# Two re-orderings in a fused attention + FFN kernel: x transposes in 64-token halves, and a second numerator among the gate/up chunks

## The chip, the cores and the metric

The kernel runs on one core of a Trainium2 chip. The metric is the device time of one execution in microseconds (us), lower is better; the figure given is the median of three runs. TensorE (PE) does the matmuls and, as a matmul against an identity, transposes; its weight loads are listed separately as PEld. VectorE (DVE), ScalarE (ACT) and GpSimd (POOL) do the elementwise work; SyncE (SP) issues DMAs in order.

## The reference

With x of 2048 tokens by 640 channels, 32 heads of 20 channels:

```
g   = sigmoid((x * gate_w).sum(-1))
q,k,v = x @ wqkv;  pq = q @ w_phi,  pk = k @ w_phi          (per head)
phi(y) = concat(softmax(y), softmax(-y))                     (40 features a head)
kv  = sum_s phi_k[s] v[s]^T,   z = sum_s phi_k[s]            (no mask: one state for all tokens)
o   = (phi_q @ kv) / (phi_q . z + 1e-6)
a   = o @ wo
b   = (gelu(x @ w_gate) * (x @ w_up)) @ w_down               (F = 1728)
out = g * a + (1 - g) * b
```

All tensors are bf16, sums are kept in f32 in PSUM.

## The kernel before

The 2048 tokens are 16 tiles of 128 tokens, and 4 blocks of 4 tiles. PSUM has 8 banks; the order of the work on each engine is written out by hand, and a small recording layer (`_Sched`) puts in the semaphore waits that the reads and writes of each operation ask for. Nothing is reordered by a planner: an engine's program order is the order in which the Python code calls it.

The stages, in the order in which PE goes through them:

1. **Start (`attention_state`, lines 544 to 572).** Seven matmuls on a constant, then the transposes of the first x block. The four tiles of that block are loaded token-major into `xtok` by two DMAs of two tiles each (line 216). `x_transpose` (line 289) transposes one tile: five PE transposes of 128 tokens by 128 channels (line 293) into one PSUM bank, then one copy to `xT`, on DVE (line 301) or ACT (line 299). Tiles 0 to 3 use banks 6, 7, 2, 3 and are copied by DVE, ACT, DVE, DVE. Then `v_step` (line 363) makes the value projection of these four tiles, one 128-row slice of `wv` at a time: for each slice and tile a matmul of 480 and one of 160 columns (line 366). It writes bank t and bank 4 or 5. The five slices of `wv` come by five DMAs (line 236), queued on SP behind the two of `xtok`.
2. **Attention state (up to line 621).** The feature weights are folded into the projections, and keys, values and queries of all tiles are made; `gram` sums the state over tiles.
3. **Gate/up (`gateups`, line 791).** For each block 14 chunks of 128 FFN channels. A chunk is 5 matmuls of 512 columns for gate and 5 for up (line 354), then gelu on ACT (line 642) and the product on DVE (line 644). Two pairs of banks, (0,1) and (6,7), alternate.
4. **Down (`downs`, line 797).** For each block two pairs of tiles (`down_pair`, line 705). A pair sums `hT @ w_down` and `goT @ wo` of two tiles in the two 64-row halves of the array at the same time: half r works on tile r first and then on the other tile, so that no two halves write one bank at once. In the first half of a pair ("opening") row r goes over all 14 down chunks and the 5 `wo` chunks of its tile, for each of the column parts of the output, in the second ("closing") over 13 down chunks and the 5 `wo` chunks of the other tile. A step (a `yield`) is two matmuls, one a half.

Between these steps stand the **numerators**: `num(t)` (line 660) makes the attention output of tile t. It is 20 matmuls of 88 columns in 64-row halves (line 670) into banks 2 to 5, then eleven DVE operations (lines 686 to 699) and a transposing DMA on SP from `Og` to `goT` (line 702). The `wo` matmuls of tile t wait for that DMA. In gate/up the DVE operations of a numerator stand in DVE's program order between two products of line 644, and these set free the banks that PE writes next.

In the kernel before, `num(0)` stands after the fifth chunk of the second gate/up block (`first_nums`, line 819). `num(1)` to `num(5)` stand in the first down block, after its steps 1, 31, 61, 91 and 121; the other three down blocks hold 4, 4 and 2 numerators at steps 1, 31, 61, 91. The first pair of the first block has an order of its own (`late`, line 766): all down legs of both halves come first, and the `wo` legs of all column parts last. There, a leg that enters a bank waits on the semaphore that the leg of the other half raises when it leaves it (`enter`, `leave`, `("turn", bk)` in line 728 and 729).

Of the kernel before, what the change touches and what calls it, by code (L numbers as in the profile page):

```python
# [3 lines left out]
P = 128  # L4
BF16 = mybir.dt.bfloat16
F32 = mybir.dt.float32
AF = mybir.ActivationFunctionType
# [100 lines left out]
class _Kernel:  # L108
# [6 lines left out]
    NFC = 14  # L115
# [170 lines left out]
        for s in range(self.NSV):  # L286
            pool(lambda e, s=s: e.memset(self.vaug[:, s, :, DH:self.DA], 1.0), [("vone", s)])

    def x_transpose(self, t, b, ek):
        sc = self.sc  # L290
        pv = self.bank(b).bitcast(BF16)
        for c in range(self.KD):
            sc.op("pe", lambda e, c=c: e.transpose(
                pv[:, c * P:(c + 1) * P], self.xtok[:, t, c * P:(c + 1) * P], self.ident[:, :]),
                reads=[("xtok", t), "ident"], writes=[("ps", b)], signal=(c == self.KD - 1))
        out = self.xT[:, :, t * P:(t + 1) * P]
        src = pv[:, 0:self.D].rearrange("p (c t) -> p c t", t=P)
        if ek == "a":
            sc.op("act", lambda e: e.activation(out, src, AF.Copy), reads=[("ps", b)], writes=[("xT", t)])
        else:  # L300
            sc.op("dve", lambda e: e.tensor_copy(out, src), reads=[("ps", b)], writes=[("xT", t)])

    def blockdiag(self):
        DH = self.DH
# [239 lines left out]
    def attention_state(self):  # L544
        NT = self.NT
        order = [(b, i) for b in range(self.NB) for i in range(self.KD)]
        sc = self.sc
        ones = self.nc.const_aps.tensor(1.0, [P, 512], BF16)
        for n in (512, 512, 512, 512, 512, 512, 128):
            sc.op("pe", lambda e: e.matmul(self.bank(0, n), ones[:, 0:P], ones[:, 0:n], start=True, stop=True),  # L550
                  writes=[("ps", 0)])
        vs, ve, xt = self.v_step, self.v_first_evac, self.x_transpose
        xt(0, 6, "d")
        xt(1, 7, "a")
        xt(2, 2, "d")
        xt(3, 3, "d")
        for t in range(4):
            vs(t, 0)
        for t in range(4):
            vs(t, 1)  # L560
        for t in range(4):
            vs(t, 2)
        for t in range(4):
            vs(t, 3)
        self.blockdiag()
        self.gate_column(6)
        for t in range(4):
            vs(t, 4)
            ve([t], "ad"[t % 2], False)
            if t == 2:  # L570
                ve([0, 1, 2], "a", True)
        ve([3], "d", True)
        f = self.fold
        ve, ke = self.v_early, self.k_early
        ve(4, 6)
        ve(5, 0)
        f(0, "k", (2, 3), "d")
        f(1, "k", (4, 5), "a")
        f(2, "k", (6, 7), "d")
        f(3, "k", (0, 1), "a")  # L580
        f(4, "k", (2, 3), "d")
        ve(6, 4)
        ke(0, 6)
        self.k_sums(0)
        ve(7, 0)
        ke(1, 2)
        f(0, "q", (4, 5), "d")
        f(1, "q", (6, 7), "d")
        ke(2, 0)
        f(2, "q", (4, 5), "d")  # L590
        f(3, "q", (2, 3), "d")
        self.proj(3, 640, 384, 6, 128, ["wk2"])
        f(4, "q", (4, 5), "d")
        self.proj(3, 1024, 257, 7, 0, ["wk2", "wgate"])
        self.k_evac(3, 6)
        self.k_scale(0)
        self.k_norm(1)
        self.pq(0, 1, 1, 0)
        self.pq(0, 0, 0, 1)
        self.pq(0, 3, 3, 2)  # L600
        self.columns = True
        self.gram(0)
        self.k_norm(2)
        self.pq(0, 2, 2)
        self.k_norm(3)
        n = 4
        g = 1
        for t in range(4, NT):
            if t < 8:
                self.k_early(t, 1)  # L610
            else:
                self.vk(t)
            self.k_norm(t)
            m = 2 * t - 2 if t < 8 else t + 5
            while n < m:
                if n == m - 1:
                    for g in range(g, t - 2):
                        self.gram(g)
                    g = t - 2
                self.pq(order[n][0], order[n][1], n)  # L620
                n += 1
# [80 lines left out]
        sc.dma("sp", lambda e: e.dma_start_transpose(self.goT[:, gs, :, :], self.Og[:, sl, :]),  # L702
               reads=[("Og", sl)], writes=[("goT", gs)], guard=old)

    def down_pair(self, t0, banks, widths, late):

        sc = self.sc
        ts = (t0, t0 + 1)
        NFC, KD = self.NFC - 1, self.KD
        nw = len(widths)  # L710
# [1 line left out]
        last = t0 + 2 == self.NT  # L712
        os_ = t0 % 4

        def mm(r, j, h, c, start, stop, enter, leave):
            t = ts[j]
            tt, gs, bk, w0, a = t % 4, t % 8, banks[h][j], sum(widths[:h]), 64 * r
            w = widths[h]
            if c <= NFC:
                lhs, rhs = self.hT(hk, c)[a:a + 64, tt * P:(tt + 1) * P], self.wd_sb[a:a + 64, c, w0:w0 + w]  # L720
                rd = [("hT", hk, c), "wd"] if c < NFC else [("hT", hk, 13, r), ("wd13", r)]
            else:
                k = c - NFC - 1
                lhs, rhs = self.goT[a:a + 64, gs, k, :], self.wo_sb[a:a + 64, k, w0:w0 + w]
                rd = [("goT", gs), "wo"]
            sc.op("pe", lambda e: e.matmul(self.bank(bk, w), lhs, rhs, start=start, stop=stop,  # L726
                                           skip_group_check=True),
                  reads=rd, writes=[("ps", bk)] + ([("turn", bk)] if leave else []), signal=leave,
                  after=[("turn", bk)] if enter else ())

        def evac(h):
            w0, w = sum(widths[:h]), widths[h]
# [18 lines left out]
                   reads=[("outsb", os_ + j, k) for j in (0, 1) for k in hs], writes=[("out", t0, h)])  # L751

        wos = [NFC + 1 + k for k in range(KD)]
        down = (list(range(NFC + 1)), list(range(NFC)))

        def leg(h, half, cs, first, fin, enter, leave):

            for x, c in enumerate(cs):
                for r in (0, 1):
                    mm(r, (r, 1 - r)[half], h, c, first and x == 0, fin and x == len(cs) - 1, enter and x == 0,  # L760
                       leave and x == len(cs) - 1)
                if fin and x == len(cs) - 1:
                    evac(h)
                yield None

        if late:
            for half in (0, 1):
                for h in range(nw):
                    yield from leg(h, half, down[half], half == 0, False, half == 1, True)
            for h in range(nw):  # L770
                yield from leg(h, 0, wos, False, False, True, True)
                yield from leg(h, 1, wos, False, True, True, True)
        else:
            for h in range(nw):
                yield from leg(h, 0, down[0], True, False, False, False)
            for h in range(nw):
                yield from leg(h, 0, wos, False, False, False, True)
            for h in range(nw):
                yield from leg(h, 1, down[1] + wos, False, True, True, True)

    NUMB = 2
    oldk = [("Ek", k, r) for k in range(4) for r in (0, 1)] + [(w, k) for w in ("Dk", "Rk") for k in range(4)] + [
# [3 lines left out]
    def ffn(self):  # L786
        self.gn = 0
        self.pn = 0
        pairs = [(0, 1), (6, 7)]

        def gateups(b, after):
            for idx, c in enumerate([0, 1, 13] + list(range(2, 13))):
                self.gateup(b, c, pairs[self.pn % 2])
                self.pn += 1
                after(idx)

        def downs(b, side):
            p = [pairs[(self.pn + k) % 2] for k in (0, 1)]
            n = 0
            for t in (4 * b, 4 * b + 2):  # L800
                final = t + 2 == self.NT
                for _ in self.down_pair(t, p + [(2, 3)] if final else p, (256, 256, 128) if final else (320, 320),
                                        t == 0):
                    n += 1
                    if n in side:
                        self.num(side[n])

        def state(idx):
            if idx < 3:
                self.gram(13 + idx)  # L810
            if idx == 2:
                self.columns = False
                self.kv_evac()
                self.gates()
                self.kv_ones()
            if 6 <= idx < 11:
                self.kv_mask(idx - 6)

        def first_nums(idx):
            if idx == 4:  # L820
                self.num(0)

        def none(idx):
            pass
        at = (1, 31, 61, 91, 121)
        nums = ((1, 2, 3, 4, 5), (6, 7, 8, 9), (10, 11, 12, 13), (14, 15))
        gateups(0, state)
        gateups(1, first_nums)
        gateups(2, none)
        gateups(3, none)  # L830
        for b in range(self.NB):
            downs(b, dict(zip(at, nums[b])))


def bass_gated_mix__linear_kernel_hedgehog__geglu_ffn__prompt_kernel(
# [41 lines left out]
```

## Time and profile before

| | us |
|---|---|
| median of three runs (290.58 to 292.26) | 290.98 |
| the profiled execution | 290.58 |
| its span, first to last instruction | 289.2 |
| PE busy (98% of the span) | 283.3 |
| DVE busy (61%) | 175.1 |
| ACT busy (36%) | 104.6 |
| down matmuls of line 726, `w_down` part, 320 columns, x648 | 48.8 |
| numerator matmuls of line 670, x320 | 9.0 |
| first transposes, line 293, x20 | 2.0 |

Rows of the profile read: the line of the kernel, the engine, the operation, what is written from what, and the tile shape; then the busy time. Matmuls overlap in the array, so the mean time of one (296 ns for a matmul of 320 columns) is longer than the time from the start of one to the start of the next. "Idle before" names the wait that ended last before an instruction started. The table of windows gives each engine's busy time and number of instructions in a stretch of the span.

### The profile page before, as it was taken

How to read it: one execution, taken by the hardware profiler on the slowest of the kernel's cores; microseconds unless marked ns; L12 is line 12 of the kernel's file. 1: busy time of each engine (PE TensorE's matmuls, PEld its weight loads, DVE VectorE, ACT ScalarE, POOL GpSimd, SP SyncE). 2: the span in 40 equal slices, each digit the busy share in tenths (PEclk: the TensorE clock that was granted, in tenths of full speed). 3: DMA queues.
4: the chain of work that ended last, by engine and by line, in shares of the span. 5: the costliest groups of instructions: out<-in, count | busy, mean ns of one | idle time of the engine just before them, and what ended most of it. 6: DMA issues, size and time to landing. Idle time of an engine off the chain costs nothing. (4 is left out here: it accounts for less than half of the span.)

```text
span 289.2 us, 7022 instructions
## 1 busy us (share of the span) xinstructions
PE 283.3 (98%) x3032; PEld 186.3 (64%) x3032; DVE 175.1 (61%) x353; ACT 104.6 (36%) x199; POOL 5.3 (2%) x36
## 2 busy tenths in 40 slices
PE   8999999999999999999999999999889999999996
PEld 4666799999984444444444444446557777777785
DVE  2359999999976644643232324236686884884801
ACT  3367888667844233222332232320112022022021
POOL 7000000000000000000000000000000000000000
DMA  7999996000002000010000000000221322532221
GB/s 225 204 184 215 370 366 196 2 0 2 0 2 48 0 0 0 3 24 0 2 0 0 0 2 0 0 0 2 48 71 25 93 44 74 70 43 76 70 71 48
DMA packets 36937, 18.67 MB, mean 65 GB/s; under 512 B 28970, under 2 KB 36394, under 8 KB 36906
## 3 DMA queue, kind: packets, MB, share of 16 engines
q1 hardware_dynamic: 36240, 18.19, 25.8%
q8 instruction: 24, 0.39, 0.6%
q10 hardware_dynamic: 666, 0.03, 0.2%
q14 instruction: 7, 0.06, 0.1%
HBM read 9.04 MB, written 2.62 MB: 40 GB/s over the span
## 5 line engine op out<-in xcount | busy, mean ns | idle before, releaser
L354 PE MATMUL ps<-xT,wg_sb 128*128 128x512 bf16 (+1 forms) x270 | 64.9, 379 | 0.0
L354 PE MATMUL ps<-xT,wu_sb 128*128 128x512 bf16 (+1 forms) x270 | 64.8, 379 | 0.0
L642 ACT ACTIVATE gl<-ps 128x512 bf16<-128x512 f32 x52 | 30.9, 597 | 72.4 <-PE ps L354 70.3
L644 DVE TENSOR_TENSOR hT<-ps,gl 128x512 bf16<-128x512 f32 x39 | 26.8, 691 | 41.9 <-PE ps L354 41.9
L726 PE MATMUL ps<-wd_sb,hT 64*128 64x320 bf16 x648 | 48.8, 296 | 0.0
L354 PEld LDWEIGHTS ps<-xT,wu_sb 128*128 128x128 bf16 (+1 forms) x270 | 26.6, 99 | 29.7 <-DVE hT L644 0.5
L354 PEld LDWEIGHTS ps<-xT,wg_sb 128*128 128x128 bf16 (+1 forms) x270 | 26.3, 99 | 29.2 <-ACT gl L642 0.2
L739 ACT ACTIVATE outsb<-ps,Gm 128x320 bf16<-128x320 f32 (+2 forms) x31 | 14.6, 516 | 76.4 <-PE ps L726 76.4
L354 PE MATMUL ps<-w,xT 128*64 128x512 bf16 (+6 forms) x400 | 41.9, 325 | 0.0
L726 PEld LDWEIGHTS ps<-wd_sb,hT 64*128 64x128 bf16 x648 | 31.4, 94 | 12.1 <-issue 0.4
L354 PEld LDWEIGHTS ps<-w,xT 128*64 128x64 bf16 (+1 forms) x400 | 35.9, 107 | 4.5
L726 PE MATMUL ps<-wo_sb,goT 64*128 64x320 bf16 (+2 forms) x340 | 27.4, 288 | 2.5 <-DMA goT<-Og 2.3
L354 PE MATMUL ps<-xT,wq 128*64 128x512 bf16 (+1 forms) x185 | 26.2, 380 | 0.0
L431 DVE TENSOR_REDUCE Dk<-Ek 128x64 f32<-128x1280 bf16 x16 | 23.7, 1479 | 3.6 <-ACT gcol L419 3.6
L445 DVE TENSOR_TENSOR Ek<-Ek,Dk 128x640 bf16<-128x640 bf16 x32 | 25.0, 821 | 0.6
L697 DVE TENSOR_TENSOR O<-ps,RH 128x640 bf16<-128x640 f32 x32 | 24.7, 815 | 0.0
L416 ACT ACTIVATE Ek<-ps 128x640 bf16<-128x640 f32 x32 | 20.7, 702 | 4.2 <-PE ps L354 4.2
L530 ACT ACTIVATE Eq<-ps 128x512 bf16<-128x512 f32 x40 | 21.6, 606 | 0.6 <-PE ps L354 0.4
L726 PEld LDWEIGHTS ps<-wo_sb,goT 64*128 64x128 bf16 x340 | 16.0, 94 | 8.9 <-DMA goT<-Og 3.0
L644 DVE TENSOR_TENSOR xT<-ps,gl 128x512 bf16<-128x512 f32 x13 | 9.0, 692 | 18.2 <-PE ps L354 18.2
L354 PEld LDWEIGHTS ps<-xT,wq 128*64 128x64 bf16 (+1 forms) x185 | 15.4, 108 | 2.8
L726 PE MATMUL ps<-wd_sb,xT 64*128 64x320 bf16 (+2 forms) x270 | 16.0, 269 | 0.0
(69 smaller groups left out, 174.2 us busy)
## 6 DMA issues: line engine op xcount, KB each, us to landing
out_dram<-outsb SPq DMA_DIRECT2D x7, 320.0 KB, 2.3
wd_sb<-in_B_w_down_dram SPq DMA_DIRECT2D x1, 2080.0 KB, 12.8
wg_sb<-in_B_w_gate_dram SPq DMA_DIRECT2D x1, 1120.0 KB, 6.1
wu_sb<-in_B_w_up_dram SPq DMA_DIRECT2D x1, 1120.0 KB, 9.5
wg_sb<-in_B_w_gate_dram SPq DMA_DIRECT2D x1, 960.0 KB, 9.6
wu_sb<-in_B_w_up_dram SPq DMA_DIRECT2D x1, 960.0 KB, 9.9
w<-in_A_wqkv_dram SPq DMA_DIRECT2D x5, 160.0 KB, 3.7
wo_sb<-in_A_wo_dram SPq DMA_DIRECT2D x1, 800.0 KB, 8.5
```

What stands on the lines that cost most here:

```text
L354: self.sc.op("pe", lambda e: e.matmul(self.ps[a:z, bank * 512 + c0:bank * 512 + c0 + n], lhs[:, a:z], rhs, start=first, stop=fin), reads=r ...
L416: self.sc.op("act", lambda e, s=s, scale=scale: e.activation(self.Ek[:, se, s, :], self.ps[:, o:o + self.D], AF.Exp, scale=scale), reads=[ ...
L431: sc.op("dve", lambda e: e.tensor_reduce(self.Dk[:, se, 0, :].rearrange("p (s h) -> p s h", h=H), self.Ek[:, se, :, :].rearrange("p s (h d ...
L445: sc.op("dve", lambda e, v=v, r=r: e.tensor_tensor(v, v, r, ALU.mult), reads=[("Rk", se)], writes=[("Ek", se, s)])
L530: sc.op("act", lambda e, s=s, scale=scale: e.activation(self.Eq[:, s, i, b * self.BT:(b + 1) * self.BT], self.bank(bank), AF.Exp, scale=sc ...
L642: sc.op("act", lambda e: e.activation(self.gl[:, slot, :], self.bank(banks[0]), AF.Gelu_apprx_tanh), reads=[("ps", banks[0])], writes=[("g ...
L644: sc.op("dve", lambda e: e.tensor_tensor(hT, self.bank(banks[1]), self.gl[:, slot, :], ALU.mult), reads=[("ps", banks[1]), ("gl", slot)], ...
L697: dve(lambda e, o=o, f=f, s=s: e.tensor_tensor(o, V[s][:, :, :, 0:DH], f, ALU.mult), rb + [key(6 + s)], [("O", s, sl)], guard=old)
L726: sc.op("pe", lambda e: e.matmul(self.bank(bk, w), lhs, rhs, start=start, stop=stop, skip_group_check=True), reads=rd, writes=[("ps", bk)] ...
L739: sc.op("act", lambda e: e.activation(dst, self.bank(bk, w), AF.Copy, scale=g), reads=rd, writes=wr)
```

## The change

There are two edits.

- `x_transpose` makes ten transposes a tile in place of five. Each takes 64 tokens by 128 channels, on one half of the array's rows; the two halves of a tile write two neighbouring PSUM banks. Tiles 0 to 3 use the bank pairs (0,1), (4,5), (2,3), (6,7). One copy per tile reads both banks. Tile 3 is copied by ACT in place of DVE.
- `num(1)` stands after the ninth chunk of the second gate/up block. The first down block holds `num(2)` to `num(5)` at steps 1, 31, 61, 91, and its first pair has the order of all other pairs; the order named `late` is gone, and with it the legs. For the other pairs the order of the matmuls is the same as before.

```
-    def x_transpose(self, t, b, ek):
+    def x_transpose(self, t, ek):
         sc = self.sc
-        pv = self.bank(b).bitcast(BF16)
+        b, w = (0, 4, 2, 6)[t], self.D // 2
+        bks = (b, b + 1)
+        pv = self.bank(b, 1024).bitcast(BF16).rearrange("p (r c) -> p r c", r=2)[:, :, 0:w]
         for c in range(self.KD):
-            sc.op("pe", lambda e, c=c: e.transpose(
-                pv[:, c * P:(c + 1) * P], self.xtok[:, t, c * P:(c + 1) * P], self.ident[:, :]),
-                reads=[("xtok", t), "ident"], writes=[("ps", b)], signal=(c == self.KD - 1))
-        out = self.xT[:, :, t * P:(t + 1) * P]
-        src = pv[:, 0:self.D].rearrange("p (c t) -> p c t", t=P)
+            for r in (0, 1):
+                a = 64 * r
+                sc.op("pe", lambda e: e.transpose(
+                    pv[:, r, c * 64:(c + 1) * 64], self.xtok[a:a + 64, t, c * P:(c + 1) * P],
+                    self.ident[a:a + 64, a:a + 64]),
+                    reads=[("xtok", t), "ident"], writes=[("ps", bks[r])], signal=(c == self.KD - 1))
+        out = self.xT[:, :, t * P:(t + 1) * P].rearrange("p c (r t) -> p c r t", t=64)
+        src = pv.rearrange("p r (c t) -> p c r t", t=64)
...
-        xt(0, 6, "d")
-        xt(1, 7, "a")
-        xt(2, 2, "d")
-        xt(3, 3, "d")
+        xt(0, "d")
+        xt(1, "a")
+        xt(2, "d")
+        xt(3, "a")
...
-        if late:
-            for half in (0, 1):
-                for h in range(nw):
-                    yield from leg(h, half, down[half], half == 0, False, half == 1, True)
-            for h in range(nw):
-                yield from leg(h, 0, wos, False, False, True, True)
-                yield from leg(h, 1, wos, False, True, True, True)
-        else:
...
+        opening = list(range(NFC + 1)) + wos
+        for part in (range(NFC + 1), range(NFC + 1, len(opening))):
+            for h in range(nw):
+                for x in part:
+                    for r in (0, 1):
+                        mm(r, r, h, opening[x], True, x, len(opening))
+                    yield None
+        closing = list(range(NFC)) + wos
+        for h in range(nw):
+            for x, c in enumerate(closing):
                 for r in (0, 1):
-                    mm(r, (r, 1 - r)[half], h, c, first and x == 0, fin and x == len(cs) - 1, enter and x == 0,
-                       leave and x == len(cs) - 1)
-                if fin and x == len(cs) - 1:
+                    mm(r, 1 - r, h, c, False, x, len(closing))
+                if c == closing[-1]:
                     evac(h)
...
         def first_nums(idx):
-            if idx == 4:
-                self.num(0)
+            if idx in (4, 8):
+                self.num(idx // 4 - 1)
...
-        at = (1, 31, 61, 91, 121)
-        nums = ((1, 2, 3, 4, 5), (6, 7, 8, 9), (10, 11, 12, 13), (14, 15))
+        at = (1, 31, 61, 91)
...
-            downs(b, dict(zip(at, nums[b])))
+            downs(b, {at[k]: 4 * b + 2 + k for k in range(4 if b < 3 else 2)})
```

More of the change, by code (lines that the diff above doesn't have):

```diff
@@ L287, in loads @@
             pool(lambda e, s=s: e.memset(self.vaug[:, s, :, DH:self.DA], 1.0), [("vone", s)])
-    def x_transpose(self, t, b, ek):
+    def x_transpose(self, t, ek):
         sc = self.sc
-        pv = self.bank(b).bitcast(BF16)
+        b, w = (0, 4, 2, 6)[t], self.D // 2
+        bks = (b, b + 1)
+        pv = self.bank(b, 1024).bitcast(BF16).rearrange("p (r c) -> p r c", r=2)[:, :, 0:w]
         for c in range(self.KD):
-            sc.op("pe", lambda e, c=c: e.transpose(
-                pv[:, c * P:(c + 1) * P], self.xtok[:, t, c * P:(c + 1) * P], self.ident[:, :]),
-                reads=[("xtok", t), "ident"], writes=[("ps", b)], signal=(c == self.KD - 1))
-        out = self.xT[:, :, t * P:(t + 1) * P]
-        src = pv[:, 0:self.D].rearrange("p (c t) -> p c t", t=P)
+            for r in (0, 1):
[6 more added lines that the diff above has]
+        src = pv.rearrange("p r (c t) -> p c r t", t=64)
+        rd = [("ps", b) for b in bks]
         if ek == "a":
-            sc.op("act", lambda e: e.activation(out, src, AF.Copy), reads=[("ps", b)], writes=[("xT", t)])
+            sc.op("act", lambda e: e.activation(out, src, AF.Copy), reads=rd, writes=[("xT", t)])
         else:
-            sc.op("dve", lambda e: e.tensor_copy(out, src), reads=[("ps", b)], writes=[("xT", t)])
+            sc.op("dve", lambda e: e.tensor_copy(out, src), reads=rd, writes=[("xT", t)])
     def blockdiag(self):
@@ L703, in num, with down_pair @@
                reads=[("Og", sl)], writes=[("goT", gs)], guard=old)
-    def down_pair(self, t0, banks, widths, late):
+    def down_pair(self, t0, banks, widths):
         sc = self.sc
@@ L713, in down_pair, with mm @@
         os_ = t0 % 4
-        def mm(r, j, h, c, start, stop, enter, leave):
+        def mm(r, j, h, c, opens, x, n):
             t = ts[j]
             tt, gs, bk, w0, a = t % 4, t % 8, banks[h][j], sum(widths[:h]), 64 * r
-            w = widths[h]
+            w, end = widths[h], x == n - 1
             if c <= NFC:
@@ L725, in mm @@
                 rd = [("goT", gs), "wo"]
-            sc.op("pe", lambda e: e.matmul(self.bank(bk, w), lhs, rhs, start=start, stop=stop,
+            sc.op("pe", lambda e: e.matmul(self.bank(bk, w), lhs, rhs, start=opens and x == 0, stop=end and not opens,
                                            skip_group_check=True),
-                  reads=rd, writes=[("ps", bk)] + ([("turn", bk)] if leave else []), signal=leave,
-                  after=[("turn", bk)] if enter else ())
+                  reads=rd, writes=[("ps", bk)] + ([("turn", bk)] if end else []), signal=end,
+                  after=[("turn", bk)] if x == 0 and not opens else ())
         def evac(h):
@@ L753, in down_pair @@
         wos = [NFC + 1 + k for k in range(KD)]
-        down = (list(range(NFC + 1)), list(range(NFC)))
-        def leg(h, half, cs, first, fin, enter, leave):
-            for x, c in enumerate(cs):
+        opening = list(range(NFC + 1)) + wos
[8 more added lines that the diff above has]
+            for x, c in enumerate(closing):
                 for r in (0, 1):
-                    mm(r, (r, 1 - r)[half], h, c, first and x == 0, fin and x == len(cs) - 1, enter and x == 0,
-                       leave and x == len(cs) - 1)
-                if fin and x == len(cs) - 1:
+                    mm(r, 1 - r, h, c, False, x, len(closing))
+                if c == closing[-1]:
                     evac(h)
                 yield None
-        if late:
-            for half in (0, 1):
-                for h in range(nw):
-                    yield from leg(h, half, down[half], half == 0, False, half == 1, True)
-            for h in range(nw):
-                yield from leg(h, 0, wos, False, False, True, True)
-                yield from leg(h, 1, wos, False, True, True, True)
-        else:
[L774 to L779, printed above, removed]
     NUMB = 2
@@ L801, in downs @@
                 final = t + 2 == self.NT
-                for _ in self.down_pair(t, p + [(2, 3)] if final else p, (256, 256, 128) if final else (320, 320),
-                                        t == 0):
+                for _ in self.down_pair(t, p + [(2, 3)] if final else p, (256, 256, 128) if final else (320, 320)):
                     n += 1
```

## The prediction

> **What bounds the kernel now.** I read the page first, for the engines' shares and the chain that ended last, then the table of windows over the stretches that the edits touch, then the waits of the worst stretch, and last the timeline at the two places where work is added.
>
> From the page:
>
> ```profile
> PE 283.3 (98%) x3032; PEld 186.3 (64%) x3032; DVE 175.1 (61%) x353; ACT 104.6 (36%) x199; POOL 5.3 (2%) x36
> PE   8999999999999999999999999999889999999996
> PE 25%; DMA 1%; issue 0%; DVE 0%; ACT 0%; SPq 0%
> ```
>
> PE is busy for 98% of the span. The two slices marked 8, late in the row, lie in the first down block; the chain that ended last begins there, with a DMA in it. The windows: the gate/up stretch with `num(0)`, the same length of gate/up without one, and down blocks 0, 1 and 2.
>
> ```profile
> 115.92:125.31 9.39, 9.39 (x61) 4.17 (x60) 6.45 (x15) 2.39 (x4) 0.00 (x0) 1.00 0.06 13
> 125.31:133.94 8.63, 8.63 (x41) 3.92 (x40) 2.77 (x4) 2.39 (x4) 0.00 (x0) 1.00 0.04 9
> 196.63:222.00 25.37, 22.90 (x397) 16.14 (x397) 19.12 (x55) 2.84 (x6) 0.00 (x0) 1.00 0.18 41
> 222.00:244.01 22.01, 21.97 (x381) 15.85 (x377) 16.36 (x46) 3.78 (x8) 0.00 (x0) 1.00 0.31 69
> 244.01:265.68 21.67, 21.67 (x380) 15.84 (x376) 15.46 (x44) 3.79 (x8) 0.00 (x0) 1.00 0.38 62
> ```
>
> The second figure is the length, the third PE's busy time. The three down blocks do the same down and `wo` matmuls; block 0 has five numerators, the others four. Block 0 takes 25.37 us and has PE idle for 2.47 of it; block 2 takes 21.67 with no idle time. The waits between 196 and 222 us say why:
>
> ```profile
> PEld ps L726 <- DMA goT<-Og: 3.0, 2, 1.7
> PE ps L726 <- DMA goT<-Og: 2.3, 2, 1.4
> PEld ps L726 <- PE ps L726: 0.8, 2, 0.4
> ```
>
> Twice PE waits for a transposed numerator, and twice for its own legs (the "turn" waits of the late order). The start, from the timeline:
>
> ```profile
> 3.81 1.84 PEld L293 LDWEIGHTS ps<-ident,xtok 128*128 128x128 bf16 x20 [0.73 <-DMA xtok<-in_A_x_dram]
> 4.56 0.49 DVE L301 COPY xT<-ps 128x640 bf16<-128x640 bf16 x1 [4.56 <-PE ps L293]
> 5.10 0.70 ACT L299 ACTIVATE xT<-ps 128x640 bf16<-128x640 bf16 x1 [2.80 <-PE ps L293]
> 5.58 0.89 DVE L301 COPY xT<-ps 128x640 bf16<-128x640 bf16 x2 [0.52 <-PE ps L293]
> 5.66 4.59 PE L366 MATMUL ps<-w,xT 128*128 128x480 bf16 x32
> ```
>
> The transposes fill PE from 3.81 to 5.66; the starts of single transposes lie 107 ns apart up to 5.28 us and 56 ns from 5.38 on, so PE ran at half speed until then. (The granted clock reads 1.00 throughout and does not show this; the spacing does.) Line 366 then runs, but for 0.22 us at 6.52, where tile 3 waits for DVE's last copy.
>
> **Edit 1: numerators and the first pair.** It removes from block 0 the fifth numerator and the late order, and makes it a block like block 2: numerators at the same four steps, the same legs.
>
> - Block 0: 25.37 to 21.67, a gain of 3.70. By parts: 0.39 for the 20 numerator matmuls (x20 take 0.39 in the chain of waits), 2.6 at the two goT waits (the gaps between starts are 1.26 and 1.66 instead of 0.14), 0.5 at the two turn waits (0.36 and 0.39 instead of 0.14); 0.2 stays unassigned.
> - Would the goT waits come back elsewhere? The first pair now needs `goT` of tiles 0 and 1 at step 29, and both are made in gate/up, over 50 us earlier. The second pair needs tile 3 at step 102, from the numerator at step 31; block 2 has just this distance and no wait. SP's queue is as in block 2 too: three transposes, the pair's output, one transpose, the next output. Nothing is late next.
> - Block 1: 22.01 to 21.67, a gain of 0.34. Its first numerator waits about 0.2 us today, because `num(5)` at step 121 still has DVE reading the banks; at step 91 it is over in time, as before block 2.
> - `num(1)` after the ninth chunk: a cost. DVE's eleven operations last about 4.2 us and stand between two products, on which PE's banks wait. The same insertion at the fifth chunk is in the trace: 9.39 against 8.63, that is 0.76, of which 0.39 is matmuls, the rest the gaps at entry and exit and a wait of 0.16 for the late product. Ends: 0.39 if nothing waits, 1.5 if the wait were paid twice over. I take 0.76, the identical row: four chunks later the banks 2 to 5 and the DVE are free again.
>
> Sum: -3.70 - 0.34 + 0.76 = -3.28.
>
> **Edit 2: transposes in halves.** 40 transposes of 64 columns replace 20 of 128. If the halves run side by side, a pair takes half of 107 ns, some 53; if one after the other, 107 and nothing is won. No row shows a transpose in halves; the nearest are matmuls in halves: 20 of line 670 with 88 columns take 0.39 us, 39 ns a pair, and 60 of line 726 with 320 columns 4.08, 136 ns a pair. Both are the time of one half. I take 53.
>
> Then tiles 0 and 1 are done at 3.81 + 10 x 0.053 = 4.34. The second half of `xtok` is issued at 1.3 and takes 3.4 to land: about 4.7, so PE waits 0.35, a wait that the slower transposes hide now. Tiles 2 and 3 go from 4.70 to 5.23. From the start of a tile's last transpose to its copy is 0.35 today, 0.30 with 64 columns. DVE copies tile 0 from 4.32 to 4.81, ACT tile 1 from 4.59 to 5.29, DVE tile 2 from 5.21 to 5.70, ACT tile 3 from 5.48 to 6.18. Line 366 begins when `wv`'s first slice is in (issued 1.73, landing in 3.6: 5.33) and bank 4, now one of tile 1's, is free (5.29): at about 5.36, not 5.66. Three tiles at 0.27 each bring it to 6.17, and tile 3 is copied at 6.18: it starts at 6.22, not 6.52. Gain: 0.30. So half of the 0.9 us saved on PE goes to DMA and copies.
>
> Bounds: the gain is 0.6 if PE is still cold all through and cold matmuls also move up; it is a loss of 0.4 if the halves do not overlap (tile 3 then sits behind ACT's slower copy, 0.1) and the copy out of two banks goes at 0.77 us, as the f32 copies of line 347, not 0.49 (0.28). I take 0.30.
>
> It should last to the end: up to 118 us PE shows no gap between matmuls beyond 0.31 us, and the DMAs next in need land earlier than wanted by more than 0.3 (`wkT` at 12.4 for 13.9, `wqT` at 20.1 for 21.1).
>
> On the clock the skill speaks against this edit. "TensorE: Matmul & The Clock Gate" (What's actually happening; PE-mode transpose) has the clock rise after a busy window of about 3.4 us whose phase is free-running, and says that transposes hardly count as busy. The trace opens at 5.28, with transposes in 1.5 us of such a window, so they cannot have kept it shut; by the rule a thinner window could hold the clock down one window longer, and an estimate from the page's 3.4 us at half speed is 1.7 us lost, a sum of -1.9 and not -3.6.
>
> **Sum.** -3.28 - 0.30 = -3.58. The profiled execution took 290.58 (span 289.2 and 1.38 around it): 287.0. The median shown is 0.40 above it, so 287.4 for a median; I predict 287.3.
>
> **Rivals.**
>
> 1. *The clock opens later.* PE has more gaps between 3.8 and 5.3 us. At 107 against 56 ns, a microsecond of cold work costs 0.48. For: the switch came only at 5.28, late in a stretch of near-unbroken work. Against: a gap of 0.35 stood before the transposes already (3.46 to 3.81), and it opened 1.5 us later. If the cold stretch grows by what it has after 3.81 (1.5 us) up to its whole length since the first matmul (0.84 to 5.28, 4.4 us), 0.7 to 2.1 are lost: 288.1 to 289.5. It decides the sign at 7.5 us of delay (3.58 / 0.48), and makes the kernel slower beyond 0.5% (1.45 us) at 10.5. That is the case on the other side, about 292.5, if the clock stays down through line 366 and the folds.
> 2. *The start gains nothing.* The halves run one after the other, or the copies bind: -3.28 to -2.88, so 287.7 to 288.1.
> 3. *The gate/up numerator costs more, or a wait stays in block 0.* For: DVE is the queue in which the added work stands, and PE does wait for it once today. At 1.5, with block 0 like block 1 (22.01): 288.5. Against: block 2 and `num(0)` are the same code in the same state.
>
> **How the numbers follow.** My forecast has 0.70, rival 1 in its mild form 0.10, rival 2 0.10, rival 3 0.05, rival 1 in its long form or another loss that turns the sign 0.03, and 0.02 for a net near zero. The range reaches from 286.3 (the start at -0.6, the gate/up numerator at 0.39, against the profiled execution) to 289.1 (rival 1 with 3.5 of its 1.5 to 4.4 us, which takes in rivals 2 and 3). Half a percent, 1.45 us, is about what runs of this kernel can tell from no change, as the three runs spread over 1.7. Faster by more than that holds for all cases to 289.5: 0.93; the same 0.03; slower 0.04.
>
> **What would show it.** After: the first down block at 21.6 to 21.8 us, no wait of line 726's successor for `goT` and none for its own legs; block 1 at the same length; gate/up with two stretches that are 0.76 longer than their neighbours; first transposes some 53 ns a pair with a gap before tile 2; the value projection beginning near 5.4. The prediction is wrong if PE waits for `goT` in the first two blocks, if the spacing of the value projection's matmuls is still that of the cold clock after 6 us, or if a product on DVE holds PE for more than half a microsecond.

## The result and the profile after

The changed kernel takes 287.74 us (median of six executions, 286.75 to 288.62) against 290.93 (six, 290.58 to 292.26) before: a ratio of 0.9883, interval 0.9851 to 0.9915. The forecast was 287.3 in a range of 286.3 to 289.1. The profiled execution took 288.32, with a span of 287.1; before it was 290.58 and 289.2. The six executions fall into two groups, three up to 287.26 and three from 288.21 on, so the median of 287.74 lies where no execution does.

The windows of the changed kernel, with the columns of the table shown of before: gate/up from `num(0)` to `num(1)`, and down blocks 0, 1 and 2.

```profile
119.80:129.04 9.24, 9.24 (x61) 4.26 (x60) 6.45 (x15) 2.39 (x4) 0.00 (x0) 1.00 0.09 20
198.76:220.43 21.67, 21.67 (x377) 15.85 (x378) 16.16 (x45) 2.84 (x6) 0.00 (x0) 1.00 0.28 48
220.43:242.10 21.67, 21.67 (x380) 15.85 (x376) 15.46 (x44) 3.79 (x8) 0.00 (x0) 1.00 0.29 63
242.10:263.77 21.67, 21.67 (x380) 15.85 (x376) 15.46 (x44) 3.79 (x8) 0.00 (x0) 1.00 0.29 63
```

Blocks 0 and 1, once 25.37 and 22.01, now take 21.67 each, with PE never idle. The matmuls' waits over the whole span are two, and neither is for `goT` (nor is any wait of the weight loads):

```profile
PE ps L557 <- PEq L856: 0.8, 1, 0.8
PE ps L298 <- DMA xtok<-in_A_x_dram: 0.4, 1, 0.4
```

The start, from the timeline (line 298 is the transposes, 308 and 306 the copies, 373 the value projection, 361 the next projections):

```profile
3.74 0.71 PE L298 MATMUL ps<-ident,xtok 64*128 64x64 bf16 x20
4.33 0.49 DVE L308 COPY xT<-ps 128x640 bf16<-128x640 bf16 x1 [4.33 <-PE ps L298]
4.59 0.70 ACT L306 ACTIVATE xT<-ps 128x640 bf16<-128x640 bf16 x1 [2.30 <-POOL mask L270]
4.87 0.71 PE L298 MATMUL ps<-ident,xtok 64*128 64x64 bf16 x20 [0.41 <-DMA xtok<-in_A_x_dram]
5.52 6.41 PE L373 MATMUL ps<-w,xT 128*128 128x480 bf16 x32
12.91 2.88 PE L361 MATMUL ps<-w,xT 128*128 128x512 bf16 x20
```

The pairs of transposes start 53 ns apart, the copies take 0.49 and 0.70, and the wait for `xtok` has appeared, all as forecast. But the first 32 matmuls of the value projection take 6.41 us, where before they took 4.59: their starts lie 0.40 us apart after 480 columns up to 9.2 us and 0.20 after 9.6. In this execution the clock opened at about 9.4 us, not 5.3, and the next projections begin 1.68 later than before (12.91 against 11.23).

From the starts of matmuls in the two traces the whole difference is: up to the first `gram` +1.68; from the last `gram` to the first down matmul +0.44 (112.16 to 112.60); from there to the last matmul -4.02 (89.97 to 85.95); from the last matmul to the end of the span -0.22 (2.59 to 2.37). The sum is -2.12, the difference of the spans 2.1. So this execution shows a start that lost and blocks that gained; three questions are open: does the late clock belong to the edit, what in edit 1 gives the 4.0, and what changed at the very end.

### The profile page after: what moved, and what is told of

Its sections match the earlier page's. It is cut to its first block, busy times and chain, and to the rows that moved or that the text cites. A ratio compares the mean times of both kernels' runs of the same rounds, so it can differ in the third digit from the quotient of the medians.

```text
span 287.1 us, 7065 instructions
## 1 busy us (share of the span) xinstructions
PE 283.6 (99%) x3052; PEld 186.7 (65%) x3052; DVE 174.5 (61%) x352; ACT 105.3 (37%) x200; POOL 5.3 (2%) x36
## 4 chain that ended last, share of the span: by engine, by line
PE 98%; DMA 1%; SPq 0%; ACT 0%; issue 0%
PE ps L361 61%; PE ps L733 28%; PE ps L373 3%; PE ps L677 2%; PE ps L468 2%; DMA xtok<-in_A_x_dram 1%; PE ps L341 1%; PE ps L298 0%; SPq L216 0%; ACT outsb L746 0%; PE ps L323 0%
## 5 line engine op out<-in xcount | busy, mean ns | idle before, releaser
L733 PE MATMUL ps<-wo_sb,goT 64*128 64x320 bf16 (+2 forms) x340 | 26.5, 288 | 0.0
## 6 DMA issues: line engine op xcount, KB each, us to landing
wg_sb<-in_B_w_gate_dram SPq DMA_DIRECT2D x1, 960.0 KB, 10.1
wu_sb<-in_B_w_up_dram SPq DMA_DIRECT2D x1, 960.0 KB, 10.1
```

## Experiments

Theory A: the halves leave gaps in PE's work before the clock opens, and with enough gaps it opens later. Theory B: the opening falls anywhere, whatever the transposes are. "Late" below is an execution 1.3 us or more above the median of the earlier group of the same kernel. Times of opening are read from the starts of single matmuls: 107 ns apart for 128 columns (400 for 480) while the clock is low, 56 (202) after.

### Each edit alone

Edit 1 alone: the changed kernel with the old `x_transpose` and its calls.

```
...
-        xt(0, "d")
-        xt(1, "a")
-        xt(2, "d")
-        xt(3, "a")
+        xt(0, 6, "d")
+        xt(1, 7, "a")
+        xt(2, 2, "d")
+        xt(3, 3, "d")
```

> Edit 1 alone (numerators and the first pair's order; the transposes as in the kernel before). Both theories: down blocks 0 and 1 at 21.67 us each, 4.0 less than before, and about 0.5 more in gate/up. Theory A (the halves thin out PE's work before the clock opens, and so it opens later in many executions): the clock opens near 5.3 us here as in the kernel before, the times lie close together, median 287.4 (290.93 - 3.5), at most one in six late by 1.7. Theory B (the opening falls where it will, whatever the transposes): the times spread from 287.0 to 288.7 as the changed kernel's do, median near 287.7 or above.

Measured: 287.91 median (287.75 to 288.46, five executions), before 291.49 beside it; ratio 0.9881 (0.9866 to 0.9896). Down blocks 0 and 1 are 21.67 each, and the stretch from `gram` to down is 0.58 longer. So edit 1 alone brings 3.6 us, and no execution is late. The clock opened at 6.55 in its profile, not near 5.3:

```profile
3.93 2.32 PE L293 MATMUL ps<-ident,xtok 128*128 128x128 bf16 x20 [0.27 <-DMA xtok<-in_A_x_dram]
6.04 4.80 PE L366 MATMUL ps<-w,xT 128*128 128x480 bf16 x32
```

So the opening does move from execution to execution, as theory B has it, but not to 9 us. The median was missed by 0.5; part of that turns out below to be at the end of the span.

Edit 2 alone: the kernel before with the new `x_transpose`.

> Edit 2 alone (transposes in halves; numerators and pairs as in the kernel before). Theory A: half or more of the executions open the clock only near 9 us and lose up to 1.7: times from 290.6 to 292.4, median above 291.3, slower than before by 0.2 to 0.4%. Theory B: the value projection starts 0.15 to 0.3 earlier and nothing else changes: median 290.7, spread as in the kernel before.

Measured: two groups, 288.32 to 289.05 (five) and 290.81, 290.94 (two); median 288.82, ratio 0.9924 (0.9897 to 0.995). The profiled execution is one of the late ones, with the opening at 10.1 us:

```profile
3.85 1.51 PE L298 MATMUL ps<-ident,xtok 64*128 64x64 bf16 x40 [0.18 <-DMA xtok<-in_A_x_dram]
5.62 6.70 PE L373 MATMUL ps<-w,xT 128*128 128x480 bf16 x32 [0.26 <-DMA w<-in_A_wqkv_dram]
```

The two groups are there, as A says, but the lower one was not expected: 2.7 us below the kernel before, on an edit that I had priced at 0.3. The profile holds part of the reason: block 0, still in the late order, takes 24.20 here and 25.37 in the kernel before, since the transposed numerators land sooner (3.3 us after the issue in place of 4.2 for the first). From the first `gram` on, the profile is 1.85 shorter than that of before (0.16 in gate/up, 1.47 in the down blocks, 0.22 at the end of the span). Taken from 290.58 this gives 288.7, which lies in the lower group. The landing times are taken up at the end.

The changed kernel once more, in two sets:

> The changed kernel once more, for more executions beside the others and a second profile. Theory A: two groups, near 286.8 and near 288.4, and the profile in the one or the other by its opening of the clock (5.3 or 9 us). Theory B: the same spread without groups, and the same spread in the kernels beside it.

> The changed kernel, for more executions beside those of the filled one. Theory A: a late group of about one in three, at 288.2 to 288.7, the others at 286.5 to 287.3. Theory B: the same distribution as the filled kernel.

Measured: 286.79 (286.56 to 287.05, and one of 288.64) and 288.16 (286.37, 286.68, and four from 288.09 to 288.68). With the first six, 17 executions fall into 9 from 286.37 to 287.26 (median 286.75) and 8 from 288.09 to 288.68 (median 288.37), with nothing between. The profiles fit: the one at 286.58 has the clock open before its second half of transposes (29 ns a pair from 4.70 on), the ones at 288.32 and 288.68 open at 9.4 and 9.7. The start of the one at 286.58:

```profile
3.80 1.33 PE L298 MATMUL ps<-ident,xtok 64*128 64x64 bf16 x40
5.66 4.53 PE L373 MATMUL ps<-w,xT 128*128 128x480 bf16 x32 [0.53 <-DVE xT L308]
11.38 2.67 PE L361 MATMUL ps<-w,xT 128*128 128x512 bf16 x19
```

### Is it the gaps that keep the clock down?

First the gaps filled with constant matmuls, whose results nothing reads:

```
-        for n in (512, 512, 512, 512, 512, 512, 128):
+        for n in (512, 512, 512, 512, 512, 512, 384):
...
         xt(1, "a")
+        sc.op("pe", lambda e: e.matmul(self.bank(7, 512), ones[:, 0:P], ones[:, 0:512], start=True, stop=True),
+              writes=[("ps", 7)])
         xt(2, "d")
```

> The changed kernel with PE's two gaps filled: the last constant matmul has 384 columns in place of 128, and one more constant matmul of 512 columns (0.43 us cold) stands between the transposes of tiles 1 and 2, in the wait for the second half of xtok. Theory A: the clock opens early again, near 5.3, and the kernel takes 286.5 to 287.0 with little spread. Theory B: no effect on the opening; median 287.7 and the spread of the changed kernel.

> The changed kernel with the two gaps filled (one constant matmul of 384 in place of 128 columns, one of 512 in the wait for xtok), for more executions. Theory A: again none in the late group, median 286.7. Theory B: one in three at 288.2 or more.

Measured: 286.70 (286.47 to 287.04) and 286.99 (286.84 to 287.09), eight executions, none late; ratios 0.9836 (0.9822 to 0.985) and 0.984 (0.9816 to 0.9864). The clock opened before 4.0 and near 5.7. This is how the first of them looks:

```profile
4.00 0.47 PE L298 MATMUL ps<-ident,xtok 64*128 64x64 bf16 x20 [0.24 <-DMA xtok<-in_A_x_dram]
4.40 0.39 PE L562 MATMUL ps<-const-bfloat16-1.0 128*128 128x512 bf16 x1
5.32 4.57 PE L373 MATMUL ps<-w,xT 128*128 128x480 bf16 x32
```

More filling: seven constants of 512 columns, 512 and 256 between tiles 1 and 2, 256 ahead of the value projection (`fill(n)` is one constant matmul of n columns).

```
...
+        fill(512)
+        fill(256)
         xt(2, "d")
         xt(3, "a")
+        fill(256, 1)
```

> The changed kernel with PE kept at work through nearly all of the start: seven constant matmuls of 512 columns (the last had 128), 512 and 256 columns more in the wait for the second half of xtok, 256 more before the value projection. Theory A (a window with too many gaps leaves the clock closed for one window more): no execution in the late group, times within 0.7 of each other near 286.7, the clock open before 6.6 us. Theory B (the late opening has nothing to do with gaps): as the changed kernel, about one execution in three is 1.5 to 2 us later than the others.

Measured: 286.89 (286.71 to 286.95, and one of 287.69). The clock opened near 5.0. None late, though the spread is 1.0 and not 0.7; no better than the smaller fill. In all, 13 executions with filled gaps hold none at 288 or above, beside 8 of 17 of the changed kernel and 2 of 7 of edit 2 alone (10 of 24). If the 10 late ones had fallen anywhere among these 37 executions, all 10 would miss the 13 with a chance of about half a percent. That speaks against theory B for the late group. One thing stays open beside it: the kernel before, which has no halves, spreads from 290.52 to 292.62 in its 40 executions, with five from 292.26 on. Only one of them was profiled, at 290.58, so whether its clock opens late at times, or its waits for `goT` vary, is not shown.

Then the other way: gaps without halves. Edit 1 with the old transposes, and two constants in place of seven.

```
-        for n in (512, 512, 512, 512, 512, 512, 128):
+        for n in (512, 512):
```

> Edit 1 with the transposes as before, and two constant matmuls of 512 columns in place of six and one of 128: PE idles from about 1.7 to 3.8 us and then transposes in full height without a gap. Theory A: the idle time makes the clock open later than in the kernel with all seven, in some or all executions: profile open at 7 us or later, median 288.4 to 289.6 against 287.9. Theory B (half-height transposes keep the clock down, gaps do not): no change, median 287.9, opening by 6.6.

Measured: 289.04 (288.07 to 289.81, six), 1.1 above edit 1 alone; ratio 0.9924 (0.9908 to 0.9941). The clock opened at 8.7 us, and the value projection's first 32 matmuls show it:

```profile
3.90 2.31 PE L293 MATMUL ps<-ident,xtok 128*128 128x128 bf16 x20 [2.05 <-DMA xtok<-in_A_x_dram]
6.01 5.86 PE L366 MATMUL ps<-w,xT 128*128 128x480 bf16 x32
```

So in this profile idle time ahead of the transposes alone, with full-height work after it, went with a late opening.

Do half-height transposes also count for less? Each was made twice, which closes the gaps with half-height work.

```
-        for c in range(self.KD):
+        for c in [c for c in range(self.KD) for _ in (0, 1)]:
```

> The changed kernel with each half-height transpose made twice: PE's work on the transposes is as long as with full height (20 pairs more, 1.06 us cold), all of it half-height. Theory A1 (gaps keep the clock down): the gaps are closed, no execution is in the late group, median 287.3 to 288.0 as edit 1 alone. Theory A2 (half-height work counts as little work): one execution in three or more late by 1.5 to 2, as in the changed kernel.

Measured: 287.46 (287.06 to 287.84, four), none late. That fits gaps alone (A1), but four executions without a late one would happen by chance about one time in nine, and the profiled one had opened by about 4.0, ahead of nearly all of the transposes. Whether the height of the work counts too stays open.

### What in edit 1 gives the 4.0 us

The changed kernel with the late order put back (`down_pair` as before, `num(1)` still in gate/up):

> The changed kernel with the first pair's late order put back; num(1) stays in gate/up. If the waits for goT in the kernel before came from making num(1) and num(2) in time for nothing, they vanish here, and the late order alone costs its turn waits: first down block 21.67 + 0.5 = 22.2 us. Rival (the late order itself brings the goT waits, wherever num(1) stands): 23.5 or more, with a wait for goT in the list of PE's waits.

Measured, in one execution (287.51) and its profile: block 0 takes 22.21 us, and the only waits of the down matmuls in it are the two turn waits. Windows and waits:

```profile
197.42:219.63 22.21, 22.03 (x378) 15.78 (x379) 16.15 (x45) 2.83 (x6) 0.00 (x0) 1.00 0.31 47
```

```profile
PEld ps L733 <- PE ps L733: 0.8, 2, 0.4
```

The other half: the new order, but five numerators in the block.

```
-            if idx in (4, 8):
-                self.num(idx // 4 - 1)
+            if idx == 4:
+                self.num(0)
...
-        at = (1, 31, 61, 91)
+        at = (1, 31, 61, 91, 121)
+        nums = ((1, 2, 3, 4, 5), (6, 7, 8, 9), (10, 11, 12, 13), (14, 15))
...
-            downs(b, {at[k]: 4 * b + 2 + k for k in range(4 if b < 3 else 2)})
+            downs(b, dict(zip(at, nums[b])))
```

> The changed kernel with five numerators in the first down block, as before, but with the order of all other pairs: the late order is dropped and num(1) stands at step 1. The first pair's wo legs then begin at step 29, some 4.2 us after num(1), and num(1) needs about 4.2 us on DVE and 3 to 4 us of DMA after that: one wait of 3 to 4.5 us, first down block 25 to 26.5 us, no better than the 25.37 of the kernel before; gate/up 0.6 shorter than in the changed kernel. Rival (the waits of the kernel before come from the late order): first block near 22.

Measured: 291.43 in one execution; block 0 takes 27.18, longer than the 25 to 26.5 expected, because there are two waits and not one. The second, 1.1 us, is for tile 3, whose numerator moves from step 31 to step 61 when `num(1)` takes the first place:

```profile
PE ps L733 <- DMA goT<-Og: 4.4, 2, 3.3
```

So moving `num(1)` is worth about 3.5 of the 4.0 and dropping the late order then 0.5 (25.69 us from the first numerator of block 0 to that of block 1 before, 22.20 with the late order put back, 21.67 in the changed kernel). Dropping the late order without the move loses 1.5 (25.69 to 27.18). The late order had been a shelter for the fifth numerator. Each of these two kernels ran once, but the waits stand in the profiles.

### The end of the span

From the last matmul to the end of the span it is 2.59 us in the kernel before, 2.90 with edit 1 alone and 3.04 with the short warm-up, and 2.37 or 2.38 in every profile of a kernel with halves. All three long ones have the shorter PE program (20 transposes, not 40). A kernel with the old transposes and about as many PE instructions as the new ones tells length from kind:

```
-        for n in (512, 512, 512, 512, 512, 512, 128):
+        for n in (128,) * 25:
```

> Edit 1 with the transposes as before, and 25 constant matmuls of 128 columns in place of six of 512 and one of 128: the same 3200 columns, 18 more instructions on PE, about as many as the halves add. In the profiles so far the last output transfer lands after 1.9 to 2.3 us with full-height transposes and 1.6 to 1.7 with halves. Theory C (that goes with the length of PE's program): 1.6 to 1.7 here and the median 0.4 below the 287.9 of edit 1 alone. Theory D (chance of the execution, or the transposes themselves): 1.9 or more, median 287.9.

Measured: 286.72 (286.63 to 286.96, four), ratio 0.9832 (0.9808 to 0.9857), and 2.37 from the last matmul to the end: theory C. Its start:

```profile
3.85 1.64 PE L293 MATMUL ps<-ident,xtok 128*128 128x128 bf16 x20 [0.19 <-DMA xtok<-in_A_x_dram]
5.33 4.67 PE L366 MATMUL ps<-w,xT 128*128 128x480 bf16 x32
```

The list of DMA queues shows what goes with it. Of the last stretch of before, of edit 1 alone, of the changed kernel and of this one (packets, MB and share of the engines by queue; the last output transfer and its time to landing):

```profile
q8 instruction: 1, 0.02, 1.9%
out_dram<-outsb SPq DMA_DIRECT2D x1, 64.0 KB, 1.9
```

```profile
q8 instruction: 1, 0.02, 1.7%
out_dram<-outsb SPq DMA_DIRECT2D x1, 64.0 KB, 2.2
```

```profile
q1 hardware_dynamic: 561, 0.20, 26.6%
out_dram<-outsb SPq DMA_DIRECT2D x1, 64.0 KB, 1.6
```

```profile
q1 hardware_dynamic: 561, 0.20, 26.7%
out_dram<-outsb SPq DMA_DIRECT2D x1, 64.0 KB, 1.6
```

In the first two an instruction packet of 16 KB, in flight for about 0.95 us, falls among the last output transfers (0.08 us before the start of the last matmul, 0.55 after it; 0.18 after in the short warm-up); in the profiles with the short end it comes 0.5 us or more before the start of the last matmul, and has landed when the last transfer is issued. The Trainium skill, "Runtime: NRT & Kernel Launch" (Instruction fetch mechanics), says that instructions are refilled in blocks of 16 KiB, 256 instructions, and that crossing one is mostly hidden. That is the size of the packet here, and at the end of this kernel it was not hidden: the span ended 0.2 to 0.7 us later.

The numerators' transfers to `goT` say the same of the packet with many more cases. The 14 profiles hold 224 of them. In 88, no instruction packet is in flight in the first 2.56 us after the issue, and every one of these lands in 2.55 to 2.64 us. In the other 136 there is one (of 16 KB, or of 8 KB on another queue), and 108 of them take more than 3.0, up to 4.56. The last output transfer does likewise: 1.65 us in the 11 profiles in which no packet overlaps it, 1.9, 2.2 and 2.3 in the three in which one does. So the packet is very likely what lengthens the transfers beside it; moving only the packet was not tried.

The new median lies 1.2 under edit 1 alone, and the end explains 0.5 of it. In the profiles most of the rest is at the start: the folds begin at 13.70 against 14.54, with the clock open at 4.6 and not 6.55 (the rows of both starts are shown above). Whether constants in short pieces open it earlier as a rule, or four executions happened to be early, stays open.

## Why the prediction was right

The time fell near the forecast because edit 1, which is nearly all of the sum, did what was forecast. Edit 2 did not, and that the median still came within 0.5 of the forecast is partly luck, since it lies between two groups of executions. One sign that the prediction itself gave for being wrong was seen: the value projection's matmuls kept the spacing of the cold clock after 6 us, up to 9.2 in the profile.

**Edit 1, block 0 and 1: -3.70 and -0.34, right to 0.02.** 25.37 and 22.01 became 21.67 and 21.67, in the changed kernel and with edit 1 alone. The rule that made it right was to price the block by a block of the same code in the same trace, waits and all, and not by adding up waits. That the waits come back nowhere is shown by the list of PE's waits.

**`num(1)` in gate/up: +0.76 forecast, about +0.6 measured.** Between the last `gram` and the first down matmul the second numerator adds 0.58 with the old transposes (112.16 before, 112.74 with edit 1 alone) and 0.60 with the halves (112.00 with edit 2 alone, 112.60 in the changed kernel). The row taken as the price, 9.39 against 8.63, held a wait of 0.16 for the late product at `num(0)`, and the added numerator has no such wait. With the halves the wait at `num(0)` is gone too: this 0.16 belongs to edit 2, which makes the +0.44 of the changed kernel against before. Why is not shown; DVE began that numerator 1.19 us after PE did in the trace of before, and 0.81 in the changed kernel.

**Edit 1 together: -3.28 forecast, -3.58 measured alone (287.91 against 291.49).** In the profiles the terms that were priced come to -4.02 + 0.58 = -3.44.

**Edit 2: -0.30 forecast; it is the step that did not hold.** Of its parts, 53 ns a pair, the wait for `xtok` (0.41, forecast 0.35) and the copies' times were right; the value projection started 0.14 earlier in that execution, where 0.30 was forecast (`xtok` landed 0.1 later). What failed first is the assumption behind them, that the clock opens at 5.3 as in the profile of before.

Nor does the 0.30 show where the clock opens early. The first `gram` starts at 28.78 in the profile at 286.58, at 28.84 in that of before, and at 28.75 with full-height transposes and short constants, whose clock opened about as early (4.6). In the profile at 286.58 the second half of the transposes ends near 5.0, but the value projection starts only at 5.66, 0.14 after the first slice of `wv` landed (5.52). With edit 2 alone it is the same: landed at 5.49, started at 5.62. The prediction had let line 366 start 0.03 after a landing at 5.33. It also took 0.22 us at 6.52 for time lost to the copy of tile 3; that is idle time of the weight loads, and the starts of the matmuls lost 0.05 there.

Against edit 1 alone (287.91) the changed kernel is 1.2 faster in about half of its executions (286.75) and 0.5 slower in the others (288.37). In the profiles at 287.91 and 286.58 the 1.3 between them is 0.65 up to the first `gram`, with the clock open at 6.55 against under 4.7, 0.14 in gate/up and 0.53 at the end of the span. The mean over the 17 is about -0.4, near the forecast, but by luck and not by its working.

**Rival 1, the clock.** I gave it 0.10 in its mild form; 8 of 17 executions were late, and the two of them that were profiled had the clock open at 9.4 and 9.7. The price was right, 1.68 at the first `gram` in the profile, inside the 0.7 to 2.1 that the rival was given. The argument against it, that a gap of 0.35 stood there already, was weak: it counted one gap and not the sum of the gaps. The Trainium skill, "TensorE: Matmul & The Clock Gate" (What's actually happening), gives a free-running window of about 3.4 us, and the estimate of 1.7 lost that I took from it is near the 1.68 measured. On that page's remark that transposes do not count as busy in the same way (PE-mode transpose), the runs speak against it: with edit 1 alone the clock opened at 6.55, after 2.1 us of transposes from 3.93 to 6.04 and 0.5 of projection, and if the window is the page's 3.4 us, only about a quarter of it was other work. How full a window has to be is not shown.

**Rivals 2 and 3.** The mechanisms of rival 2 fell: the halves do run side by side, and the copies out of two banks cost no more. Its outcome, a start that gains nothing, is nevertheless what the profiles with an early clock show. Rival 3 fell: the gate/up numerator cost less than its row, and no wait stayed in block 0.

**What no case held:** the end of the span, 0.2 to 0.5 shorter with the longer PE program. It helped the sum against the late clock: -4.02 + 0.44 + 1.68 - 0.22.

**The versions beside each other.** The changed kernel with filled gaps (286.70 and 286.99) and edit 1 with full-height transposes and 25 short constants (286.72) take what the changed kernel takes where its clock opens early, and have none late in 12 executions. Both beat the kernel before by 1.6%; the halves are not needed for it.

## What to carry to other kernels

Price a stretch that is to become like another by that other stretch of the same trace, and look for the one thing in it that is not alike; here it gave 4.0 us to two hundredths. Shortening PE's work in the first microseconds can cost more than it saves: here the shorter transposes then waited for DMAs, and with these gaps the clock opened late, or so their times say, in 10 of 24 executions, with the gaps filled in none of 13. Read the spacing of matmul starts, not the granted clock, to see it. When a few instructions more or less change the time of an unrelated place, look at where the instruction packets lie among the transfers.

## What was not expected of the hardware

- The clock's opening moved between executions, from about 4.0 or earlier to 6.55 us in seven profiles of kernels that keep PE at work, and in seven of kernels with gaps it was found either under 5.8 (three) or at 8.7 to 10.1 (four). The granted clock of the profile read 1.00 in all of them.
- An instruction packet of 16 KB among the last output transfers went with a landing of 1.9 to 2.3 us, in place of 1.65 without it.
- The same numerator transfer took 4.2 us to land in the kernel before and 3.3 with edit 2 alone. A packet of 16 KB overlaps it in both, from 2.1 and from 0.8 us after the issue. Without a packet these transfers take 2.55 to 2.64; by an estimate from that, the first wait of block 0 would not have been there (issued at 201.82, landed by 204.5, needed at about 204.8). So the kernel before, whose order waits for these transfers, depends on where the packets fall. With the order of the changed kernel the stretch from the first down matmul to the last took 85.95 in all ten profiles.
